# Linear attention with a mixture of adapters: v copied with a one behind each token, and sums of 65 columns instead of 128

## The chip, the cores and the metric

The kernel runs on one core of a Trainium2 chip. The metric is the device time of one execution in microseconds (us). Below, PE is the matrix engine, DVE, ACT and POOL are the vector, scalar and GpSimd engines, SP is the engine that issues the stores.

## The reference

The program computes a linear ("cosformer") attention for 8 batches, 8 heads, 576 tokens and head size 64, and sends its output, as a matrix of 4608 tokens by 512, through a mixture of 8 low-rank adapters of which each token takes two:

```
q_p = concat(relu(q) * cos_w, relu(q) * sin_w)      # 128 features a head
k_p = concat(relu(k) * cos_w, relu(k) * sin_w)
kv  = einsum('bhsf,bhsd->bhfd', k_p, v)
z   = sum over s of k_p
x   = einsum(q_p, kv) / (einsum(q_p, z) + 1e-06)    # x: (4608, 512)
logits = x @ w_gate;  topk = two best of 8;  w = softmax over the two
out = x + sum over the chosen e of w_e * (x @ A[e]) @ B[e]
```

## The kernel before, in words

A batch has 576 tokens as 64 rows of 9 slots s; two heads of 64 rows each fill the 128 partitions, so k, q and v of a batch are tiles of 128 x (4 head pairs, 9 slots, 64). Work is staged by a loop over 36 token tiles n of 128 tokens (`for n in range(NT - 1)`, L511), each of two slots of a batch; nine tiles make two batches, and the fifth of nine mixes both (`mixed`). The order of the instructions on every engine is written out by hand (`tc.manual_schedule`): in step n come, as far as they are due, `evac_x` (n-1), `normalise` (n), `move_q` (n+1), logits, the k-v sums, gates, deltas, `transp_x` (n), the k work and `numden` (n+1). Tables computed ahead (`kv_at`, `relu_at`, `pool_at`, `act_at`, `dve_at`, `gate_a_at` and so on) say which step does what.

- k: `relu_k` (L165, DVE, in place, bf16) and then `scale_k` (L156, POOL) by the cosine and the sine make `kp`, two instructions a slot. For batches 4 to 7 the relu pair and POOL's 16 or 18 instructions are issued in steps 12, 17, 20 and 23.
- k-v sums: `kv(b, s)` (L180) adds one slot of a batch to the sums in the two PSUM banks `cd`: 8 matmuls, 4 head pairs by two row halves of 64, with the 128 features of kp as weights. The moving side is 64 columns of v and 64 columns of one, which give z in 64 equal columns (`v_rhs` makes the two pieces by a jump to a block of ones behind v). `kv_out` (L188, ACT) takes 65 columns of each. For batch b the sums are spread over the steps ahead of its first tile: batches 4 to 7 in steps 14 to 17, 18 to 21, 23 to 26 and 27 to 30.
- q: `transp_q` (L213, or L201 from tile 27 on) transposes and scales q on PE, `evac_q` (L229, ACT) applies the relu.
- `numden(n)` (L247, L252) makes numerator and denominator of a tile, 65 columns a head; a first small matmul puts 1e-06 into the denominators. `normalise` (L259, L266, DVE) takes the reciprocal and multiplies into `xt`.
- `transp_x` (L274), `evac_x` (L280, DVE), `logits` (L300), `gate_a`, `gate_sig`, `gate_b`, `transp_z` (L348), `delta` (L366, L371) and `evac_o` (L397) are the adapters, in groups of three tiles.

A step's DVE list is: `evac_x`, `normalise`, gates, DVE's scales, `relu_k`. A step's PE list is: `transp_q`, logits that are early, `kv`, deltas, `transp_x`, `transp_z`, late logits, `numden` of the next tile.

Of the kernel before, what the change touches and what calls it, by code (L numbers as in the profile page):

```python
# [8 lines left out]
FP32 = mybir.dt.float32  # L9
BF16 = mybir.dt.bfloat16  # L10
AF = mybir.ActivationFunctionType
ALU = mybir.AluOpType

NS = 9
HALF = 64
EPS = 1e-6
# [3 lines left out]
def kernel(ctx, tc, q, k, v, w_gate, A, Bw, out):  # L20
    nc = tc.nc
    B, H, S, D = q.shape
# [4 lines left out]
    W = D + 1  # L27
    ZW = ER + R
    DCH = DM // 128
    G = H // 2  # L30
# [3 lines left out]
    persist = ctx.enter_context(tc.tile_pool(name="persist", bufs=1))  # L34
# [128 lines left out]
    def relu_k(b, s0, s1):  # L163
        x = k_b[b][:, :, s0:s1, :].rearrange("p g s d -> p g (s d)")
        nc.vector.tensor_scalar(out=x, in0=x, scalar1=0.0, scalar2=None, op0=ALU.max)  # L165

    def v_rhs(b, g, s, pr):
        base = v_b[b][pr, (g * NS + s) * D:(g * NS + s + 1) * D]
        p, (step, n) = base.ap[0], base.ap[-1]
        jump = VN - (g * NS + s) * D  # L170
        return bass.AP(base.tensor, base.offset, [p, [jump * step, 2], [step, n]])

    kv_n = {b: 0 for b in range(B)}

    def kv(b, s):
        first, last = kv_n[b] == 0, kv_n[b] == NS - 1
        kv_n[b] += 1
        for g in range(G):
            for par, pr in enumerate((lo, hi)):
                nc.tensor.matmul(out=kvz[par][:, g], lhsT=kp_t[b][pr, s, g],  # L180
                                 rhs=v_rhs(b, g, s, pr),
                                 start=(first and g == 0), stop=(last and g == G - 1))

    def kv_out(b):
        kv_t[b] = t = p_kv.tile([128, 2, G, W], BF16, name="kvsb")
        for par in range(2):
            src = kvz[par].rearrange("p g u d -> p g (u d)")[:, :, 0:W]
            nc.scalar.copy(t[:, par], src)  # L188
# [44 lines left out]
    def move_q(n):  # L233
        transp_q(n)
        evac_q(n, 0)
        evac_q(n, 1)

    def numden(n):
        nd_t[n] = nd = ps.tile([128, 2, 512], FP32, name="nd")
        tok = tokens(n)  # L240
        if mixed(n):
            jobs = [(lo, tok[0][0]), (hi, tok[1][0])]
        else:
            jobs = [(slice(0, 128), tok[0][0])]
        for gg in range(2):
            qpT = qpT_t.pop((n, gg))
            nc.tensor.matmul(out=nd[:, gg, D:4 * W:W], lhsT=ones, rhs=eps_hi, start=True,  # L247
                             stop=False, skip_group_check=True)
            for j in range(4):
                h = 2 * j + gg if quad(n) else gg * 4 + j  # L250
                for pr, b in jobs:
                    nc.tensor.matmul(out=nd[pr, gg, j * W:(j + 1) * W],  # L252
                                     lhsT=qpT[:, j, pr], rhs=kv_t[b][:, h % 2, h // 2, :],
                                     start=False, stop=(j == 3), skip_group_check=True)

    def normalise(n):
        nd = nd_t.pop(n)[:, :, 0:4 * W].rearrange("p g (j x) -> p g j x", x=W)
        rden = p_g.tile([128, H], FP32, name="rden")
        nc.vector.reciprocal(rden, nd[:, :, :, D:W])  # L259
        xt_t[n] = xt = p_x.tile([128, DM], BF16, name="xt")  # L260
        x = xt
        if quad(n):
            x = xt.rearrange("p (g two d) -> p two g d", two=2, d=D)
        else:
            x = xt.rearrange("p (g j d) -> p g j d", g=2, d=D)
        nc.vector.tensor_tensor(  # L266
            out=x, in0=nd[:, :, :, 0:D],
            in1=rden.rearrange("p (g j) -> p g j", g=2).to_broadcast([128, 2, 4, D]),
            op=ALU.mult)
# [18 lines left out]
    def logits(n):  # L288
        g = group_of[n]
        i = n - groups[g][0]  # L290
        if i == 0:
            if g == len(groups) - 1:
                t = qd.tile([128, 512], FP32, name="zb", tag="qd")
            else:
                t = ps.tile([128, 512], FP32, name="za")
            za_t[g] = t[:, 0:3 * ZW].rearrange("p (i z) -> p i z", z=ZW)
            u_t[g] = t[:, 3 * ZW:3 * ZW + 3 * E].rearrange("p (i e) -> p i e", e=E)
        xT = xT_t.pop(n)
        for c in range(DCH):
            nc.tensor.matmul(out=za_t[g][:, i, :], lhsT=xT[:, c, :], rhs=AW[:, :, c, :],  # L300
                             start=(c == 0 and i == 0), stop=(c == DCH - 1),
                             skip_group_check=True)
# [107 lines left out]
            (eng or nc.sync).dma_start(out=dst, in_=t)  # L410


    kv_at, relu_at, pool_at, act_at, dve_at = {}, {}, {}, {}, {}

    def put(at, step, what):
        at.setdefault(step, []).append(what)
# [6 lines left out]
    for b in range(2, B):  # L423
        first = b // 2 * NS + b % 2 * 4
        at = {2: 5, 3: 8, 4: 12, 5: 17, 6: 20, 7: 23}[b]
        n_pool = {2: 5, 3: 7, 4: 8, 5: 8}.get(b, 9)
        for s0, s1 in ((0, 3), (3, n_pool)):
            put(relu_at, at, (b, s0, s1))
        for s in range(n_pool):
            put(pool_at, at, (b, s))  # L430
        for i in range(2):
            if n_pool <= 7:
                put(dve_at, at, (b, 7, i))
            if n_pool < 9:
                put(act_at, first - 4 + i, (b, 8, i))
            if n_pool == 5:
                put(act_at, first - 3 + i, (b, 6, i))
                put(act_at, first - 2, (b, 5, i))
        order = (7, 0, 1, 2, 3, 4, 8, 6, 5) if n_pool <= 7 else (0, 1, 2, 3, 4, 5, 8, 6, 7)
        if n_pool == 9:  # L440
            order = range(NS)
        for j, s in enumerate(order):

            ahead = (2 if j < 4 else 1) if b < 4 else 4 - min(j // 2, 3)
            put(kv_at, first - ahead, (b, s))


# [2 lines left out]
    prev = 5  # L450
    for g, t in enumerate(groups[:-2]):
        at = max(t[-1] + 1, prev + 1)
        if g == 1:
            at += 1
        for n in t:
            if t[-1] + 1 < at or (n < t[-1] and prev == at - 1):
                put(late_at, at - 1, n)
            else:
                put(early_at, max(n + 1, at - 1), n)
        prev = at + 1  # L460
        put(gate_a_at, at, g)
        put(gate_b_at, at + 1, g)
        put(move_at, at + 2, g)
    put(late_at, NT - 2, NT - 3)

    with tc.manual_schedule():
# [44 lines left out]
        for n in range(NT - 1):  # L511
            if n > 0:
                g = move_at.get(n - 1, (None,))[0]
                evac_x(n - 1, g)
                if g is not None:
                    todo += groups[g]
            normalise(n)
            if n != 3:
                move_q(n + 1)
            for t in early_at.get(n, ()):  # L520
                logits(t)
            for b, s in kv_at.get(n, ()):
                kv(b, s)
                if kv_n[b] == NS:
                    kv_out(b)
            if n == 3:
                move_q(n + 1)
            for g in gate_a_at.get(n, ()):
                gate_a(g)
            for g in gate_b_at.get(n, ()):  # L530
                gate_b(g)
            now = todo[:2 if len(todo) > 3 and n not in kv_at else 1]
            del todo[:len(now)]
            for d in now:
                emit(d, n not in kv_at, add=n > 27)
            for g in gate_a_at.get(n, ()):
                gate_sig(g)
            transp_x(n)
            for g in move_at.get(n, ()):
                transp_z(g)  # L540
            for b, s, i in dve_at.get(n, ()):
                scale_k1(b, s, i, "dve")
            for b, s0, s1 in relu_at.get(n, ()):
                relu_k(b, s0, s1)
            for b, s in pool_at.get(n, ()):
                scale_k(b, s)
                if (b, s) == pool_at[n][-1]:
                    if b + 3 < B:
                        load_k(b + 3)
                    if b + 2 < B:  # L550
                        load_q(b + 2)
                    if b + 3 < B:
                        load_v(b + 3)
                    if b + 3 == B - 1:

                        nc.sync.dma_start(out=first_loads, in_=k_b[B - 1][0:1, 0, 0, 0:8])
                        for d in held:
                            store(d)
                        held = None
            for t in late_at.get(n, ()):  # L560
                logits(t)
            numden(n + 1)
            for b, s, i in act_at.get(n, ()):
                scale_k1(b, s, i, "act")
# [57 lines left out]
```

## Time and profile before

| | |
|---|---|
| time, median of 3 runs | 115.53 us (115.42 to 115.57) |
| the profiled execution | 115.39 us |
| its span | 113.6 us, 5022 instructions |
| busy | PE 99.4, DVE 80.9, ACT 78.1, POOL 73.2 us |
| kv matmuls (L180) | 576, 20.1 us busy |
| HBM | 28.85 MB read, 9.44 MB written |

The page gives the busy time of each engine, then the span in 40 slices, the DMA queues, the chain of work that ended last, and the costliest groups of instructions. In a timeline row stand start, length, engine, line, operation, output<-inputs, shape and count; an instruction's length counts from its start on the engine to its end, and neighbours overlap by some tens of ns. Rows of stretches give, for each engine, busy time and number of instructions, then the granted PE clock, the DMA share and GB/s.

### The profile page before, as it was taken

The page shows a single profiled execution, that of the slowest core. Times are in us where ns is not written, and L with a number is a line of the kernel's source. Part 1 is how long each engine was busy: PE and PEld are TensorE (multiplying, and loading weights), DVE is VectorE, ACT ScalarE, POOL GpSimd, SP SyncE. Part 2 cuts the span into 40 slices and gives each one's busy share as a digit, 9 for nine tenths or more (in the row PEclk, how much of TensorE's full clock was granted, in tenths as well). Part 3 has the DMA queues.
Part 4 walks back from the last instruction along what each step waited for, and adds up shares of the span by engine and source line. Part 5 has one row for each costly group of instructions (what it writes and reads, how often), then busy time and mean ns, then how long its engine had stood idle before and what let it go on. Part 6 is the DMA issues. An engine that isn't in the chain of part 4 may idle for free.

```text
span 113.6 us, 5022 instructions
## 1 busy us (share of the span) xinstructions
PE 99.4 (88%) x2099; PEld 74.2 (65%) x2099; DVE 80.9 (71%) x280; ACT 78.1 (69%) x169; POOL 73.2 (64%) x135
## 2 busy tenths in 40 slices
PE   2999777877898999999999999999999999978710
PEld 1347566766795688777877877777877876754200
DVE  5698488559949958696767886998658478786620
ACT  5077579846995847586876958956777678895720
POOL 5991222238996994999449989989950444984000
PEclk9999999999999999999999999999999999999998
DMA  2999999999999999999999999999988122655892
GB/s 40 383 208 207 207 209 207 208 184 211 204 214 203 206 209 209 208 208 209 207 209 206 211 204 208 260 359 378 380 304 314 52 97 98 175 190 220 291 332 88
DMA packets 19671, 24.77 MB, mean 218 GB/s; under 512 B 2625, under 2 KB 14529, under 8 KB 19649
## 3 DMA queue, kind: packets, MB, share of 16 engines
q0 software_dynamic: 13856, 13.84, 73.2%
q1 hardware_dynamic: 5792, 10.62, 26.4%
q8 instruction: 16, 0.26, 0.9%
q14 instruction: 7, 0.05, 0.1%
HBM read 28.85 MB, written 9.44 MB: 337 GB/s over the span
## 4 chain that ended last, share of the span: by engine, by line
PE 52%; DMA 26%; DVE 11%; POOL 3%; issue 2%; ACT 2%; POOLq 0%; DVEq 0%; ACTq 0%
DMA k<-in_k_dram 14%; DMA v<-in_v_dram 12%; PE cd L180 10%; PE za L300 8%; PE qd L213 7%; PE nd L252 6%; PE xz L274 5%; PE dx L366 4%; DVE xt L266 4%; PE qd L201 3%; PE dx L371 3%; PE xz L348 2%; DVE zg L335 2%; DVE xT L280 2%; ACT qpT L229 1%
## 5 line engine op out<-in xcount | busy, mean ns | idle before, releaser
L229 ACT ACTIVATE qpT<-qd 128x512 bf16<-128x512 f32 x71 | 38.6, 596 | 15.2 <-PE qd L213 11.5
L156 POOL TENSOR_SCALAR kp<-k,cos_tab 128x256 bf16<-128x256 bf16 x46 | 22.5, 490 | 7.2 <-DVE k L165 6.3
L280 DVE COPY xT<-xz 128x512 bf16<-128x512 bf16 (+1 forms) x36 | 17.2, 477 | 13.7 <-PE xz L348 7.5
L266 DVE TENSOR_TENSOR xt<-nd,rden 128x512 bf16<-128x512 f32 x36 | 24.9, 691 | 1.4
L156 POOL TENSOR_SCALAR kp<-k,sin_tab 128x256 bf16<-128x256 bf16 x46 | 21.9, 476 | 0.0
L180 PE MATMUL cd<-v,kp 64*128 64x128 bf16 x576 | 20.1, 217 | 0.8 <-DMA v<-in_v_dram 0.8
L274 PEld LDWEIGHTS <-xt 128*128 128x128 bf16 x144 | 10.8, 115 | 12.0 <-DVE xt L266 7.6
L180 PEld LDWEIGHTS <-kp 64*128 64x128 bf16 x576 | 16.2, 94 | 3.4 <-issue 0.8
L252 PE MATMUL nd<-kvsb,qpT 128*128 128x65 bf16 (+1 forms) x320 | 16.9, 194 | 1.0 <-DVE qpT L231 0.5
L274 PE MATMUL xz<-ident,xt 128*128 128x128 bf16 x144 | 14.4, 222 | 3.6 <-DVE xt L266 3.6
L213 PE MATMUL qd<-diag,q 128*64 128x128 bf16 x432 | 17.2, 222 | 0.0
L391 POOL TENSOR_TENSOR osb<-osb,xt 128x512 f32<-128x512 f32 x9 | 10.2, 1160 | 9.5 <-ACT osb L397 9.0
L397 ACT COPY osb<-dx 128x512 f32<-128x512 f32 x18 | 10.6, 591 | 5.3 <-PE dx L371 5.0
L213 PEld LDWEIGHTS <-q 128*64 128x64 bf16 x432 | 12.9, 109 | 1.5 <-DMA q<-in_q_dram 0.2
L252 PEld LDWEIGHTS <-qpT 128*128 128x128 bf16 (+1 forms) x320 | 12.4, 99 | 1.7 <-ACT qpT L229 0.7
L300 PE MATMUL za<-AW,xT 128*128 128x144 bf16 x140 | 12.2, 227 | 0.6 <-DVE zg L335 0.5
L247 PE MATMUL nd<-eps_hi,ones 128*128 128x4 bf16 x72 | 11.6, 169 | 0.0
L300 PEld LDWEIGHTS <-xT 128*128 128x128 bf16 x144 | 9.1, 98 | 2.8 <-DVE xT L280 0.8
L259 DVE RECIPROCAL rden<-nd 128x8 f32<-128x8 f32 x36 | 7.2, 200 | 4.8 <-PE nd L252 4.8
L397 ACT COPY osb<-cd 128x512 f32<-128x512 f32 x17 | 9.7, 599 | 1.3 <-PE cd L371 1.3
L62 POOL DMA_DIRECT2D v<-in_v_dram x8 | 6.3, 782 | 5.1 <-DMA q<-in_q_dram 4.3
L471 PE MATMUL wu<-wide,ones 128*128 128x512 bf16 x24 | 7.7, 495 | 2.0 <-DVE AW L115 2.0
(73 smaller groups left out, 137.5 us busy)
## 6 DMA issues: line engine op xcount, KB each, us to landing
out_dram<-osb SPq DMA_DIRECT2D x32, 256.0 KB, 3.9
v<-in_v_dram POOLq DMA_DIRECT2D x8, 576.0 KB, 17.2
q<-in_q_dram POOLq DMA_DIRECT2D x8, 576.0 KB, 16.2
k<-in_k_dram POOLq DMA_DIRECT2D x7, 576.0 KB, 15.6
k0f<-in_k_dram SPq DMA_DIRECT2D x1, 1152.0 KB, 5.4
out_dram<-osb SPq DMA_DIRECT2D x8, 128.0 KB, 2.5
AW<-in_moe_A_dram POOLq DMA_DIRECT2D x1, 128.0 KB, 18.1
Ball<-in_moe_B_dram POOLq DMA_DIRECT2D x1, 128.0 KB, 16.5
```

What stands on the lines that cost most here:

```text
L156: nc.gpsimd.tensor_scalar(out=dst, in0=src, scalar1=tab, scalar2=1.0, op0=ALU.mult, op1=ALU.mult)
L180: nc.tensor.matmul(out=kvz[par][:, g], lhsT=kp_t[b][pr, s, g], rhs=v_rhs(b, g, s, pr), start=(first and g == 0), stop=(last and g == G - 1))
L213: nc.tensor.matmul(out=t[cols, j, 2 * gi:2 * gi + 2, :], lhsT=q_b[b][:, 2 * gp + gi, s, :], rhs=diag[:, s, i], start=(j == 0 and gi == 0), ...
L229: nc.scalar.activation(t, src, AF.Relu)
L247: nc.tensor.matmul(out=nd[:, gg, D:4 * W:W], lhsT=ones, rhs=eps_hi, start=True, stop=False, skip_group_check=True)
L252: nc.tensor.matmul(out=nd[pr, gg, j * W:(j + 1) * W], lhsT=qpT[:, j, pr], rhs=kv_t[b][:, h % 2, h // 2, :], start=False, stop=(j == 3), sk ...
L266: nc.vector.tensor_tensor(out=x, in0=nd[:, :, :, 0:D], in1=rden.rearrange("p (g j) -> p g j", g=2).to_broadcast([128, 2, 4, D]), op=ALU.mult)
L274: nc.tensor.transpose(out=xz[:, c * 128:(c + 1) * 128], in_=x[:, c], identity=ident)
L280: nc.vector.tensor_copy(t[:, 0:c], xz[:, 0:c * 128].rearrange("p (c s) -> p c s", c=c))
L300: nc.tensor.matmul(out=za_t[g][:, i, :], lhsT=xT[:, c, :], rhs=AW[:, :, c, :], start=(c == 0 and i == 0), stop=(c == DCH - 1), skip_group_ ...
L391: nc.gpsimd.tensor_tensor(out=t, in0=t, in1=xt_t.pop(n), op=ALU.add)
L397: nc.scalar.copy(t, src)
```

## The change

- For batches 4 to 7 DVE copies v, two or three slots at a time, into one of three tiles `v1` whose slots have 66 columns, the last two of them one (set once by POOL in step 3). The copy of tokens' slots 0-1, 2-3, 4-5 and 6-8 of batch b stands at the end of DVE's list in the steps `first - 5` to `first - 2`, where `first` is the batch's first tile: steps 13 to 16, 17 to 20, 22 to 25 and 26 to 29. The matmuls of these batches then read 65 adjacent columns and write 65 instead of 128.
- In the 16 tiles of `kv_at` beyond 13 (14 to 21, 23 to 30) the 1e-06 is no longer put in by matmuls: DVE adds it to the denominators before the reciprocal.
- The k-v sums of batch 3 are spread over steps 10 to 12 instead of 11 and 12; group 1's gate is no longer held back a step, so that groups 1 to 3 are gated one step earlier (8, 10, 12 instead of 9, 11, 13); early logits stand behind `kv` instead of ahead of it.

```diff
+    VS = D + 2
+    v1_t = [persist.tile([128, G, 3, VS], BF16, name=f"v1{i}") for i in range(3)]
+    v1_of = {}
+
+    def copy_v(b, ss):
+        t = v1_t.pop(0)
+        v1_t.append(t)
+        src = v_b[b][:, 0:VN].rearrange("p (g s d) -> p g s d", g=G, s=NS)
+        nc.vector.tensor_copy(t[:, :, 0:len(ss), 0:D], src[:, :, ss[0]:ss[-1] + 1, :])
+        for i, s in enumerate(ss):
+            v1_of[b, s] = t[:, :, i, 0:W]
+
     def kv(b, s):
...
-                nc.tensor.matmul(out=kvz[par][:, g], lhsT=kp_t[b][pr, s, g],
-                                 rhs=v_rhs(b, g, s, pr),
+                o, rhs = kvz[par][:, g], None
+                if (b, s) in v1_of:
+                    o, rhs = cd[par][:, g * 128:g * 128 + W], v1_of[b, s][pr, g]
+                else:
+                    rhs = v_rhs(b, g, s, pr)
+                nc.tensor.matmul(out=o, lhsT=kp_t[b][pr, s, g], rhs=rhs,
                                  start=(first and g == 0), stop=(last and g == G - 1))
...
+    def eps_dve(n):
+
+        return n > 13 and n in kv_at
+
     def numden(n):
...
-            nc.tensor.matmul(out=nd[:, gg, D:4 * W:W], lhsT=ones, rhs=eps_hi, start=True,
-                             stop=False, skip_group_check=True)
+            if not eps_dve(n):
+                nc.tensor.matmul(out=nd[:, gg, D:4 * W:W], lhsT=ones, rhs=eps_hi, start=True,
+                                 stop=False, skip_group_check=True)
...
-                                     start=False, stop=(j == 3), skip_group_check=True)
+                                     start=(eps_dve(n) and j == 0), stop=(j == 3),
+                                     skip_group_check=True)
...
     def normalise(n):
...
-        nc.vector.reciprocal(rden, nd[:, :, :, D:W])
+        den = nd[:, :, :, D:W]
+        if eps_dve(n):
+            den1 = p_g.tile([128, 2, 4, 1], FP32, name="den1")
+            nc.vector.tensor_scalar(out=den1, in0=den, scalar1=EPS, scalar2=None, op0=ALU.add)
+            den = den1
+        nc.vector.reciprocal(rden, den)
...
+        if b >= 4:
+            for i in range(4):
+                put(copy_at, first - 5 + i, (b, range(2 * i, 2 * i + 2 + i // 3)))
         for j, s in enumerate(order):
 
-            ahead = (2 if j < 4 else 1) if b < 4 else 4 - min(j // 2, 3)
+            if b == 2:
+                ahead = 2 if j < 4 else 1
+            elif b == 3:
+                ahead = 3 if j < 2 else 2 if j < 5 else 1
+            else:
+                ahead = 4 - min(j // 2, 3)
             put(kv_at, first - ahead, (b, s))
...
-        if g == 1:
-            at += 1
...
             normalise(n)
+            if n == 3:
+                for t in v1_t:
+                    nc.gpsimd.memset(t[:, :, :, D:], 1.0)
             if n != 3:
                 move_q(n + 1)
-            for t in early_at.get(n, ()):
-                logits(t)
             for b, s in kv_at.get(n, ()):
                 kv(b, s)
                 if kv_n[b] == NS:
                     kv_out(b)
+            for t in early_at.get(n, ()):
+                logits(t)
...
             for b, s0, s1 in relu_at.get(n, ()):
                 relu_k(b, s0, s1)
+            for b, ss in copy_at.get(n, ()):
+                copy_v(b, ss)
             for b, s in pool_at.get(n, ()):
                 scale_k(b, s)
```

More of the change, by code (lines that the diff above doesn't have):

```diff
@@ L410, in store @@
             (eng or nc.sync).dma_start(out=dst, in_=t)
-    kv_at, relu_at, pool_at, act_at, dve_at = {}, {}, {}, {}, {}
+    kv_at, relu_at, pool_at, act_at, dve_at, copy_at = {}, {}, {}, {}, {}, {}
     def put(at, step, what):
```

## The prediction

> **What bounds the kernel now.** I read the page first (busy times, slices, chain), then the busy time by stretches, then the timeline of DVE and POOL inside the longest stretch.
>
> ```profile
> PE 99.4 (88%) x2099; PEld 74.2 (65%) x2099; DVE 80.9 (71%) x280; ACT 78.1 (69%) x169; POOL 73.2 (64%) x135
> PE 52%; DMA 26%; DVE 11%; POOL 3%; issue 2%; ACT 2%; POOLq 0%; DVEq 0%; ACTq 0%
> DMA k<-in_k_dram 14%; DMA v<-in_v_dram 12%; PE cd L180 10%; PE za L300 8%; PE qd L213 7%; PE nd L252 6%; PE xz L274 5%; PE dx L366 4%; DVE xt L266 4%; PE qd L201 3%; PE dx L371 3%; PE xz L348 2%; DVE zg L335 2%; DVE xT L280 2%; ACT qpT L229 1%
> ...
> core 0: us, PE busy (x) PEld busy (x) DVE busy (x) ACT busy (x) POOL busy (x), PEclk, DMA share, GB/s
> 34.30:49.13 14.83, 14.07 (x291) 10.89 (x290) 11.56 (x44) 9.65 (x22) 12.27 (x25) 1.00 1.21 207
> 49.13:94.09 44.96, 44.65 (x1020) 35.06 (x1020) 33.94 (x106) 33.02 (x71) 33.19 (x67) 1.00 1.00 240
> ```
>
> The first 34.3 us wait for loads (the chain's DMA share). From 49.13 to 94.09, which are steps 14 to 30 of the token-tile loop, 17 steps of 2.64 us, PE is busy 44.65 of 44.96 us: PE sets the pace, and DVE has 44.96 - 33.94 = 11.0 us to spare. Everything the change adds lies in this stretch, or one step ahead of it.
>
> POOL matters too. It scales k in four unbroken runs of `scale_k`, of 16, 16, 18 and 18 instructions, each released by the `relu_k` pair of the same batch on DVE (steps 12, 17, 20, 23):
>
> ```profile
> 45.55:53.02 7.47, 7.45 (x16) 1.00 1.22 210
> 58.28:65.76 7.48, 7.44 (x16) 1.00 1.21 208
> 66.80:75.17 8.37, 8.35 (x18) 1.00 1.18 246
> 75.60:83.90 8.30, 8.24 (x18) 1.00 1.02 375
> ```
>
> One relu of the fourth batch met the end of the third run. In the timeline of DVE and POOL:
>
> ```profile
> 45.11 0.35 DVE L165 TENSOR_SCALAR k<-k 128x768 bf16<-128x768 bf16 x1
> 57.85 0.35 DVE L165 TENSOR_SCALAR k<-k 128x768 bf16<-128x768 bf16 x1
> 58.12 0.49 DVE L165 TENSOR_SCALAR k<-k 128x1280 bf16<-128x1280 bf16 x1
> 58.30 0.64 POOL L156 TENSOR_SCALAR kp<-k,cos_tab 128x256 bf16<-128x256 bf16 x1 [3.06 <-DVE k L165]
> 58.93 0.47 POOL L156 TENSOR_SCALAR kp<-k,sin_tab 128x256 bf16<-128x256 bf16 x1
> 65.83 0.81 DVE L165 TENSOR_SCALAR k<-k 128x768 bf16<-128x768 bf16 x1
> 73.77 0.48 POOL L156 TENSOR_SCALAR kp<-k,sin_tab 128x256 bf16<-128x256 bf16 x1
> 73.79 1.58 DVE L165 TENSOR_SCALAR k<-k 128x768 bf16<-128x768 bf16 x1
> 74.22 0.48 POOL L156 TENSOR_SCALAR kp<-k,cos_tab 128x256 bf16<-128x256 bf16 x1
> 74.68 0.48 POOL L156 TENSOR_SCALAR kp<-k,sin_tab 128x256 bf16<-128x256 bf16 x1
> 75.65 0.53 POOL L156 TENSOR_SCALAR kp<-k,cos_tab 128x256 bf16<-128x256 bf16 x1 [0.49 <-PE xz L348]
> ```
>
> The same relu of 768 bf16 elements takes 0.35 us when POOL is idle and 1.58 us here. It ends at 75.37, which is 0.35 us after 75.03, 0.13 before the recorded end of the last POOL instruction of the run (75.16). Two POOL instructions, at 74.22 and 74.68, started after it and went first. The other way round, the POOL instruction at 58.30 that meets a running relu takes 0.64 instead of 0.47, so it waits for that one relu and no more. I read: a bf16 DVE instruction from SBUF to SBUF and a POOL instruction exclude each other, POOL gets in between two of DVE, and DVE gets in only where POOL's run has a gap. DVE's copies out of PSUM don't take part:
>
> ```profile
> 48.88 0.62 DVE L280 COPY xT<-xz 128x896 bf16<-128x896 bf16 x1
> 59.85 0.62 DVE L280 COPY xT<-xz 128x896 bf16<-128x896 bf16 x1 [1.24 <-PE xz L348]
> 67.60 0.62 DVE L280 COPY xT<-xz 128x896 bf16<-128x896 bf16 x1 [0.50 <-PE xz L348]
> 75.76 0.61 DVE L280 COPY xT<-xz 128x896 bf16<-128x896 bf16 x1
> 91.05 0.62 DVE L280 COPY xT<-xz 128x896 bf16<-128x896 bf16 x1 [1.50 <-PE xz L348]
> ```
>
> They take the same 0.62 us inside POOL's runs (48.88) and after the last of them (91.05).
>
> **The change part by part.** *Narrower k-v sums.* 288 of the 576 `kv` matmuls (batches 4 to 7) stream 65 columns instead of 128.
>
> ```profile
> 52.95 0.55 PE cd L180 x16
> 83.87 0.43 PE qd L201 x32
> 48.67 0.17 PE L247 MATMUL nd<-eps_hi,ones 128*128 128x4 bf16 x1
> 48.70 0.28 PE L252 MATMUL nd<-kvsb,qpT 128*128 128x65 bf16 x4
> 48.82 0.17 PE L247 MATMUL nd<-eps_hi,ones 128*128 128x4 bf16 x1
> ```
>
> Today one costs 0.55/16 = 34 ns. The nearest rows bound the new one: the 64x64 matmuls with 64 columns run at 0.43/32 = 13 ns, and the numerator's 65-column matmuls with a whole 128x128 weight load at 0.15/5 = 30 ns (from 48.67 to 48.82, one eps and four of them). With half the weight rows and full columns it lies between: 22 ns, 288 x 12 = 3.5 us of PE saved (bounds 1.2 to 6.0; 0 if the weight load sets the pace).
>
> *No eps matmul* in 16 tiles (n of 14 to 21 and 23 to 30): 32 of those 30 ns, 1.0 us of PE. In exchange a `tensor_scalar` of 128x8 from PSUM, in front of the reciprocal and on the path from `numden` to `xt`: the nearest row is the reciprocal itself.
>
> ```profile
> L259 DVE RECIPROCAL rden<-nd 128x8 f32<-128x8 f32 x17 | 3.4, 198 | 0.8 <-PE nd L252 0.8
> ```
>
> 16 x 0.2 = 3.2 us of DVE. *The copies* without hindrance: by the relu at 57.85 (the next starts 0.27 later) 0.2 us for 512 elements and 0.27 for 768: 12 x 0.2 + 4 x 0.27 = 3.5 us. DVE then needs 33.9 + 3.2 + 3.5 = 40.6 us in these 17 steps, 2.39 a step, and PE 44.65 - 4.5 = 40.1. The two are level and wait for each other every step, so I count 60% of PE's 4.5 us: -2.7 us (from +3.2, the eps adds wholly exposed with no gain, to -7.0).
>
> *Copies against POOL's runs.* `copy_v` stands at the end of DVE's list of a step, behind `relu_k`; behind it stand `evac_x` and `normalise` of the next step, for which PE's `transp_x` waits, and PE's next `kv` needs the copy itself. By the reading above:
> - Step 13 (batch 4, tokens 0 and 1): DVE reaches it by about 48.9, POOL's first run lasts to 53.01. DVE is free again at 53.01 - 0.13 + 0.2 = 53.08 instead of 48.88: **4.2 us**. The copies of steps 14 to 16 find POOL without a run.
> - Step 17: relu, relu, copy. POOL's first instruction already waits when the second relu ends, takes its turn, and 16 instructions follow to 65.75. DVE is free at 65.82 instead of 59.85: **6.0 us**. By then steps 18 and 19 have no run to meet.
> - Step 20: likewise with 18 instructions and a three-token copy: 75.16 - 0.13 + 0.27 = 75.30, but here the first relu took 0.81 instead of 0.35 (POOL was writing a load's descriptors, which will long be over): 74.84 instead of 67.60: **7.2 us**.
> - Step 23: the run to 83.89; its relu no longer waits 1.23 us, so 82.73 instead of 75.76: **7.0 us**. Steps 24 to 29 are free.
>
> Together 24.4 us, all exposed: PE has only the next `transp_q` to do meanwhile.
>
> The Trainium skill ("SBUF — State Buffer", Who interferes with whom) says that such a DVE instruction and a POOL instruction lock each other out, for the whole of the one instruction that issued first. By that rule a copy would wait for one scale of 0.45 us, and the sum would be rival C's 113.9. This trace's 1.58 us, across two later POOL instructions, disagrees.
>
> *PE's clock.* Half speed shows at both ends of the trace:
>
> ```profile
> 2.00:6.77 4.77, 4.77 (x12) 1.70 (x12) 1.00 1.01 291
> 6.78:9.60 2.82, 2.82 (x14) 1.08 (x12) 1.00 1.21 208
> ...
> 108.45:112.58 4.13, 0.00 (x0) 0.00 (x0) 0.69 (x1) 0.15 (x1) 0.00 (x0) 1.00 0.71 261
> 112.60:113.60 1.00, 0.00 (x0) 0.00 (x0) 0.00 (x0) 0.00 (x0) 0.00 (x0) 0.50 0.03 8
> ```
>
> After 4.13 us without a matmul the granted clock is 0.5; and in the first 4.77 us of the warm-up twelve 512-column matmuls run where later twelve need 2.6 us. (The column says 1.00 there because no clock event precedes.) Stall 1 leaves PE idle some 3.4 us, the others 5 to 7, so three of them should drop the clock, each for about 4.8 us of work, 2.4 us lost if PE is the bound throughout. I take half, 3 x 1.2 = **3.6 us** (0 to 9.6).
>
> *The rest.* The group-1 gate a step earlier, the batch-3 sums over three steps and logits behind `kv` reorder work of steps 7 to 15: PE has 14.83 - 14.07 = 0.8 us idle from 34.3 to 49.1; I take -0.3 (+0.3 to -0.8). Three small memsets on POOL lie under the load-bound start.
>
> Sum: the profiled execution took 115.39 us (span 113.6 and 1.79 around it; the three runs' median is 115.53). 115.4 - 0.3 - 2.7 + 24.4 + 3.6 = **140.4 us**. Own range 133 to 146.
>
> **The rivals.** *B, the copy goes first behind the relus.* If DVE keeps the port between two instructions in a row, the copies of steps 17, 20 and 23 pass, and those of the steps after meet the runs: step 13 4.2, step 18 about 3.6, step 22 about 2.9, step 24 about 5.8, in all 16.5, with one or two clock drops (1.5): 115.4 - 3.0 + 16.5 + 1.5 = 130.4 (124 to 134). Against it: the start of the trace, where POOL's descriptor writing gets between DVE's back-to-back diag builds, one of which then takes 0.51 instead of 0.26 us:
>
> ```profile
> 3.86 0.76 POOL L62 DMA_DIRECT2D k<-in_k_dram  x1
> 3.96 0.26 DVE L110 TENSOR_SCALAR diag<-ident,cos_tab 128x128 bf16<-128x128 bf16 x1 [1.49 <-POOL ident masks.py:199]
> 4.13 0.51 DVE L110 TENSOR_SCALAR diag<-ident,sin_tab 128x128 bf16<-128x128 bf16 x1
> ```
>
> *C, faster: DVE gets in at the next POOL boundary.* Then a copy waits at most one POOL instruction, 0.45, on average 0.23. Some nine copies fall into runs: 2.1 us more of DVE, 42.7 us in all, so that of 44.96 at most 2.3 can be won, less by the waits: I take 1.2, 115.4 - 0.3 - 1.2 = 113.9 (112 to 117). It decides where a copy in a run takes under some 0.6 us. For it: POOL itself waited for one relu only. Against it: the 1.58 us, across two boundaries.
>
> *D, faster: the copies don't contend,* as their rows of 64 differ from the relu's long rows: 115.4 - 0.3 - 2.7 = 112.4. Against it: same type, both ends in SBUF.
>
> *E, not what it says:* 65 columns save nothing as the weight load sets the pace; inside the forecast that is 2 us more, within its range.
>
> **How the numbers follow.** Forecast 0.50, B 0.22, C 0.22, D 0.06. A difference under 0.2% (0.23 us) can't be told from none. Slower: 0.72 from the forecast and B, and 0.05 of C, 0.77; same 0.02; faster 0.15 of C and D, 0.21. The range takes nearly all of the forecast and B and half of C: 113 to 146.
>
> **What would show it.** Right: four COPY instructions v1<-v of over 4 us in steps 13, 17, 20 and 23, each ending with POOL's last scale of a run, the other twelve near 0.3; PEclk under 1 behind them; `evac_x` idle before it. B: the long copies stand in steps 18, 22 and 24. C: none over 0.8 us. The narrow sums: 16 of them in about 0.35 us. Wrong altogether: time near 113 with DVE busy over 90% from step 14 to 30.

## The result, and the profile after

The changed kernel takes 114.41 us (median of 6 runs, 114.11 to 114.68) beside 115.55 us of the kernel before on the same chip (6 runs): a ratio of 0.990, interval 0.988 to 0.992. It is faster by 1.1 us; the forecast was 140.4. The profiled execution took 114.68 us, its span is 112.9.

Busy times and slices of DVE and PEclk from the page after, and the same stretch as before from the busy times by stretches:

```profile
PE 94.1 (83%) x2050; PEld 71.1 (63%) x2068; DVE 87.2 (77%) x312; ACT 78.5 (70%) x169; POOL 73.8 (65%) x137
DVE  5599489459969676798997999999989788777410
PEclk9999999999999999999999999999999999999997
POOL 11%; PE 11%; DVE 11%; ACT 3%; issue 2%; DMA 2%; DVEq 0%; ACTq 0%
49.00:94.00 45.00, 41.41 (x1025) 32.90 (x1034) 40.77 (x141) 34.41 (x74) 37.14 (x72) 1.00 1.04 249
49.80:92.60 42.80, 39.68 (x969) 31.37 (x973) 38.84 (x135) 32.76 (x69) 35.25 (x69) 1.00 1.05 252
```

Over the whole span PE's busy time fell by 5.3 us and DVE's rose by 6.3. In steps 14 to 30 (49.80 to 92.60) DVE is busy 38.84 of 42.80 us, 91%; before it was PE that was busy 99%. PE's granted clock never dropped before the end. The chain's shares are small because it could be followed back only to 62.29.

The groups of the new instructions in that stretch, and one row of the chain with 16 narrow sums:

```profile
L199 PE MATMUL cd<-v,kp 64*128 64x65 bf16 x288 | 7.9, 191 | 0.9 <-POOL kp L156 0.6 <-issue 0.3
L183 DVE COPY v<-v 128x512 bf16<-128x512 bf16 (+1 forms) x16 | 6.6, 415 | 0.0
L286 DVE TENSOR_SCALAR den<-nd 128x8 f32<-128x8 f32 x16 | 2.4, 152 | 0.0
83.65 0.35 PE cd L199 x16
```

The narrow sums run at 0.35/16 = 22 ns, the adds cost 0.15 us each, and the copies, waits included, 0.41. Two places of the timeline where DVE meets a run of POOL:

```profile
72.14 0.48 POOL L156 TENSOR_SCALAR kp<-k,cos_tab 128x256 bf16<-128x256 bf16 x1
72.23 0.54 DVE L183 COPY v<-v 128x512 bf16<-128x512 bf16 x1
72.60 0.52 POOL L156 TENSOR_SCALAR kp<-k,sin_tab 128x256 bf16<-128x256 bf16 x1
74.05 1.42 DVE L165 TENSOR_SCALAR k<-k 128x768 bf16<-128x768 bf16 x2
```

The copy at 72.23 (0.28 bare) waits for the rest of one scale, 0.25 us, and goes first at the next boundary; the scale behind it is held instead. Even the relu pair at 74.05, whose first is the relu of the forecast's 1.58 us, now gets through. No copy waited over 0.3 us. The stalls, 24.4 of the forecast's 25 us, were not there.

Three things were left to find: whether such a stall exists at all, what made the gain, and why it was not more.

### The profile page after: what moved, and what is told of

The parts are those of the page before. It is cut to its first block, busy times and chain, and to the rows that moved or that the text cites. A ratio compares the mean times of both kernels' runs of the same rounds, so it can differ in the third digit from the quotient of the medians.

```text
span 112.9 us, 4975 instructions
## 1 busy us (share of the span) xinstructions
PE 94.1 (83%) x2050; PEld 71.1 (63%) x2068; DVE 87.2 (77%) x312; ACT 78.5 (70%) x169; POOL 73.8 (65%) x137
## 5 line engine op out<-in xcount | busy, mean ns | idle before, releaser
L156 POOL TENSOR_SCALAR kp<-k,cos_tab 128x256 bf16<-128x256 bf16 x46 | 23.3, 506 | 6.4 <-DVE k L165 6.2
L199 PE MATMUL cd<-v,kp 64*128 64x128 bf16 (+1 forms) x576 | 17.5, 204 | 1.4 <-POOL kp L156 0.6
L199 PEld LDWEIGHTS <-kp 64*128 64x128 bf16 x576 | 13.8, 94 | 4.3 <-POOL kp L156 1.1
L420 POOL TENSOR_TENSOR osb<-osb,xt 128x512 f32<-128x512 f32 x8 | 9.2, 1159 | 8.4 <-ACT osb L426 6.8
L426 ACT COPY osb<-dx 128x512 f32<-128x512 f32 x19 | 11.2, 589 | 5.0 <-PE za L329 1.9
L426 ACT COPY osb<-cd 128x512 f32<-128x512 f32 x16 | 9.1, 597 | 1.3 <-PE cd L400 1.3
L506 PE MATMUL wu<-wide,ones 128*128 128x512 bf16 x24 | 7.2, 469 | 2.0 <-DVE AW L115 2.0
L62 POOL DMA_DIRECT2D q<-in_q_dram x8 | 6.1, 758 | 3.3 <-DMA k<-in_k_dram 3.1
L62 POOL DMA_DIRECT2D k<-in_k_dram x7 | 5.4, 771 | 4.1 <-DMA k<-in_k_dram 2.4
```

The source lines that it names most:

```text
L62: eng.dma_start(out=t, in_=rows(dram, b))
L156: nc.gpsimd.tensor_scalar(out=dst, in0=src, scalar1=tab, scalar2=1.0, op0=ALU.mult, op1=ALU.mult)
L199: nc.tensor.matmul(out=o, lhsT=kp_t[b][pr, s, g], rhs=rhs, start=(first and g == 0), stop=(last and g == G - 1))
L420: nc.gpsimd.tensor_tensor(out=t, in0=t, in1=xt_t.pop(n), op=ALU.add)
L426: nc.scalar.copy(t, src)
```

## Experiments: does DVE wait for the end of POOL's run?

**The copies alone.** The kernel before with `copy_v` at the same places, its tiles read by nobody.

```diff
+            for b, ss in copy_at.get(n, ()):
+                copy_v(b, ss)
```

> The kernel before, and in it the sixteen copies of v at their steps of the change, read by nobody; nothing else changed. Theory P (the prediction's: a copy that meets one of POOL's runs waits for the run's end): copies of over 4 us in steps 13, 17, 20 and 23, time near 135 us. Theory Q (a copy gets in at the next POOL boundary, as the changed kernel's trace suggests): no copy over 0.65 us, each met one taking its bare 0.28 or 0.35 plus what is left of the running scale less 0.13; time 115.5 to 117, since DVE had 11 us to spare.

115.42 us beside 115.43, ratio 0.9992 (0.9979 to 1.0006): the 16 copies alone cost nothing. The longest:

```profile
64.35 0.68 DVE L180 COPY v<-v 128x512 bf16<-128x512 bf16 x1
```

It came 0.08 us before a boundary, missed that one and took the next. So the forecast's reading of one row was not the rule.

**The 1e-06 by PE in every tile.** The changed kernel with

```diff
-        return n > 13 and n in kv_at
+        return False
```

> The changed kernel with the 1e-06 put in by PE's matmuls again in all tiles. Theory D (DVE sets the pace): 16 additions of 0.19 us start to start leave DVE, 3.0 us, against 1.0 us more of PE: 113.0 to 114.0. Theory PE (PE still sets it): 1 us later, 115.0 to 115.6. Neither: within 0.3 us of 114.4.

116.91 us is the middle of twelve runs in two groups, six from 114.99 to 116.46 and six from 117.36 to 117.71; the ratio of 1.003 (1.000 to 1.007) is that of the lower six. What parts the groups was not followed. The profiled run, 115.71, shows the forecast's stall for the first time:

```profile
71.95 3.33 DVE L183 COPY v<-v 128x512 bf16<-128x512 bf16 x1
```

This copy of step 22 waited 3.05 us, to the end of POOL's third run. So the comparison says nothing of the 1e-06; it is done again below.

**The old order.** The changed kernel with the gate of group 1, batch 3's sums and the early logits where they were before.

```diff
+        if g == 1:
+            at += 1
...
+            for t in early_at.get(n, ()):
+                logits(t)
             for b, s in kv_at.get(n, ()):
```

> The changed kernel with the order of before in the three places: group 1 held back, batch 3's sums in two steps, early logits ahead of kv. Theory H (the new order costs some 0.5 us ahead of step 14, where the changed kernel runs 0.5 to 0.8 us behind the one before, and this reaches the end): 113.7 to 114.1. Theory H0 (what is lost there is taken up later): 114.2 to 114.6. Theory H+ (the order is what makes the later steps fit): over 114.8.

118.03 us, ratio 1.022 (1.020 to 1.024): slower than before. The timeline, and the busy times behind it:

```profile
72.10 0.47 POOL L156 TENSOR_SCALAR kp<-k,cos_tab 128x256 bf16<-128x256 bf16 x1
72.11 3.79 DVE L183 COPY v<-v 128x512 bf16<-128x512 bf16 x1
75.27 0.47 POOL L156 TENSOR_SCALAR kp<-k,sin_tab 128x256 bf16<-128x256 bf16 x1
76.28 0.66 PE L329 MATMUL za<-AW,xT 128*128 128x144 bf16 x4 [2.93 <-DVE xT L309]
76.00:79.60 3.60, 3.32 (x39) 2.40 (x41) 2.48 (x8) 0.58 (x1) 1.80 (x4) 0.53 1.02 386
```

One copy let seven later scales pass. PE stood for 2.93 us, and its granted clock averaged 0.53 in the 3.6 us from 76.00 on: the whole mechanism of the forecast, at one place instead of four.

**Where in a scale the copy arrives.** The copies of the last two runs came 0.02 and 0.00 us after the start of a scale. Here a 128x128 memset stands in front of the old order's copy of step 22.

```diff
+                if n == 22:
+                    for _ in range(1):
+                        nc.vector.memset(late[:, 0:128], 0.5)
                 copy_v(b, ss)
```

> The changed kernel in the old order, which took 118.0 us, with one memset of 128x128 bf16 on DVE (0.14 us) ahead of the copy of step 22, whose copy took 3.79 us there, having arrived 1 ns after a POOL scale began. Theory R (a copy that arrives within some 20 ns of the beginning of a scale, while two scales overlap, waits for the run's end; any other waits for the next boundary): the copy of step 22 takes under 0.6 us, no stall, 113.7 to 114.6 us, though some 0.1 us of work was added. Theory H+ (the old order itself costs it): 118.0 or a little more.

118.19 us, ratio 1.026 (1.021 to 1.032). The copy came 0.145 us into a scale and waited all the same:

```profile
72.30 3.64 DVE L185 COPY v<-v 128x512 bf16<-128x512 bf16 x1
```

The moment of arrival is not the cause. PE stood for 2.93 us here too, and its clock was halved for 3.41 us (first row); in the 1e-06 run above, where the copy left PE without a matmul for 2.55 us, the clock stayed at 1.00 (second and third row):

```profile
77.74:81.15 3.41, 3.41 (x52) 2.55 (x49) 2.94 (x13) 1.60 (x3) 3.31 (x7) 0.50 1.02 383
```

```profile
72.88:75.43 2.55, 0.00 (x0) 0.03 (x1) 2.55 (x2) 0.96 (x2) 2.25 (x5) 1.00 1.14 293
75.43:79.00 3.57, 3.57 (x81) 2.98 (x82) 3.40 (x11) 1.57 (x3) 2.00 (x5) 1.00 1.07 374
```

A second try at the moment of arrival put four small memsets ahead of step 13's copy in the kernel with the copies alone:

```diff
+                if n == 13:
+                    for _ in range(4):
+                        nc.vector.memset(late[:, 0:1], 0.5)
```

> The kernel before with the copies alone (115.42 us, no copy over 0.68 us), and four memsets of 128x1 on DVE ahead of the copy of step 13. That copy arrived 279 ns after a scale began, and scales begin every 453 to 454 ns; four memsets of 44 ns should bring it to 279 + 176 - 453 = 2 ns after the next. Theory R: it waits for the end of POOL's first run at 53.0, 3.9 us, and the time is 118 to 120. Any other arrival: at most 0.75 us, time 115.4 to 115.7.

The copy came 0.24 us into a scale of the first run, missed the aim, and took 0.38 us; one run of 115.83 us. It tells nothing more.

**POOL's descriptors ahead of the run.** Only the third run directly follows the writing of a load's descriptors (q of batch 7). This load was issued with the loads behind the first run, in the old order, in the new order without the rest of the change, in the changed kernel and in before.

```diff
-                    if b + 2 < B:
+                    if b + 2 < B - 1:
                         load_q(b + 2)
...
+                    if b == 4:
+                        load_q(7)
```

> The changed kernel with the old order, whose copy of step 22 waited 3.5 us in POOL's third run; here the last load of q (batch 7) is issued with the loads behind POOL's first run instead of between its second and third, so that POOL writes no descriptors right ahead of the third run. Theory S (the descriptors written right ahead of a run are what leaves no turn for DVE between its scales): the copy of step 22 takes at most 0.6 us, the third run's first scale is 0.64 or more as in the runs that follow an idle POOL, no granted clock under 0.99, and the time falls from 118.0 to 115.2 to 116.0. Rival (the third run starves DVE whatever stands ahead of it): the copy of step 22 takes over 3 us again, 117.8 to 118.4.

> The kernel before with the new order alone, and the same load of q issued behind POOL's first run. Theory S: the relu of step 23, which took 1.73 us in the order alone, takes at most 0.7; the wait lay partly beside other work, so the time is 113.5 to 114.1. Rival: the relu takes over 1.2 us again, and 114.0 to 114.3; or the queue's other order makes a load late, 114.5 or more with idle time of PE before step 14.

> The changed kernel with the load of q of batch 7 issued behind POOL's first run. If the new order and the narrow sums relieve the same engine, so that their gains do not add once DVE is 91% busy: within 0.3 us of the changed kernel, 114.1 to 114.7, and behind the old order with the same early load (113.87). If the early load by itself is worth something besides the stall: 113.2 to 113.8. No long wait in POOL's third run by either, as its first scale is held by a relu and a copy already.

> The kernel before with the load of q of batch 7 issued behind POOL's first run, and nothing else. If the early load is worth nothing by itself, all that the old order with copies and narrow sums won (113.87) is theirs: 115.2 to 115.7 here. If the early load carries it: 114.0 to 114.6. The relu of step 23, 1.58 us in before, may wait or not; it is not on the path of this kernel by either.

The old order gained 4.2 us, more than either theory allowed: 113.87 us, ratio 0.987 (0.985 to 0.988), and its copy of step 22 (first row below) waited 0.23 us. But with the order alone the relu of step 23 (second row) still waited 0.98 us, to the end of the run; 114.82 us, 0.993 (0.990 to 0.995). That is 0.75 us behind the order alone, but not in all runs: three of the seven lie at 114.10 to 114.18, beside the order alone, and four at 114.82 to 114.96. In the profiled run, one of the four, the tiles fall behind at steps 29 to 31, which was not followed further.

```profile
71.86 0.51 DVE L183 COPY v<-v 128x512 bf16<-128x512 bf16 x1
```

```profile
73.58 1.33 DVE L165 TENSOR_SCALAR k<-k 128x768 bf16<-128x768 bf16 x1
```

In before with the early load the same relu still waited 0.77 us. So the descriptors are not the cause, though moving them took the wait away once. The changed kernel did not move: 114.43 us, 0.992 (0.990 to 0.995), though its last tile's xt came 0.84 us earlier. Before gained 0.16 us: 115.28 us, 0.9987 (0.9978 to 0.9996).

**The hold of the run's first scale.** Where the first scale of the third run took 0.77 us or more, held by relu and copy, nothing waited long. So one kernel got a hold (the order alone, with one unread copy behind the relus of step 20), and one lost it (the changed kernel, step 20's copy ahead of the relus):

```diff
+        if b == 6:
+            put(copy_at, at, (b, range(6, 9)))
```

```diff
+            if n == 20:
+                for b, ss in copy_at[n]:
+                    copy_v(b, ss)
             for b, s0, s1 in relu_at.get(n, ()):
                 relu_k(b, s0, s1)
-            for b, ss in copy_at.get(n, ()):
-                copy_v(b, ss)
+            if n != 20:
+                for b, ss in copy_at.get(n, ()):
+                    copy_v(b, ss)
```

> The kernel before with the new order alone, and one copy of three slots of v (read by nobody) behind the relus of step 20. Theory T (in POOL's third run DVE finds no turn where the run's first scale was held by one relu or none, 0.48 to 0.66 us, and finds one at every boundary where relu and copy held it, 0.77 or more): the first scale takes 0.8 us, the relu of step 23 at most 0.7 instead of 1.73, and the time is 113.8 to 114.1. Rival (the lengths of the first scale are chance): the relu takes over 1.2 us again, 114.1 to 114.3.

> The changed kernel with step 20's copy ahead of that step's two relus instead of behind them, so that one relu alone holds the first scale of POOL's third run. Theory T: that scale takes 0.65 us, the copy of step 22 or the relu of step 23 then waits to the end of the run, 1.2 to 3.6 us, and the time is 115.0 to 118.0. Rival: no copy over 0.7 us, and the time within 0.3 us of the changed kernel's 114.4.

With the hold (0.84) the relu of step 23 waited 0.21 us, as the theory expected; 114.16 us, 0.990 (0.987 to 0.993). Without it (0.64, first row) the copy of step 22 (second row) waited under 0.1 us all the same; 114.19 us, 0.991 (0.988 to 0.994):

```profile
67.26 0.64 POOL L156 TENSOR_SCALAR kp<-k,cos_tab 128x256 bf16<-128x256 bf16 x1 [0.33 <-PE xz L377]
71.78 0.36 DVE L183 COPY v<-v 128x512 bf16<-128x512 bf16 x1
```

That theory falls too. What decides stays open. Over all 20 traces, 160 relus and copies started inside a scale with over 0.13 us of it left: 152 waited at most 0.33 us, which is at most the rest of that scale less 0.13 us; 8 waited 0.77 to 3.5 us, to the run's end, all in POOL's third run. These 8 came 0.00 to 0.32 us into a scale.

## Experiments: what made the gain, and what held it back

**The order alone.** The kernel before with the three moves of the order, and no copies, narrow sums or adds; and with the logits behind the sums alone.

```diff
-        if g == 1:
-            at += 1
...
-            for t in early_at.get(n, ()):
-                logits(t)
             for b, s in kv_at.get(n, ()):
...
+            for t in early_at.get(n, ()):
+                logits(t)
```

> The kernel before with the new order alone (group 1's gate a step earlier, batch 3's sums over steps 10 to 12, early logits behind kv); no copies, sums of 128 columns, eps on PE. By the comparison of xt's starts, where the changed kernel is 0.5 us late at steps 12 and 13: 115.8 to 116.2. If the order pays later on (kv_out earlier): 115.0 to 115.4.

> The kernel before with the early logits behind the k-v sums, and nothing else of the new order. If this edit makes the order's gain of 1.4 us (PE has the sums to do while DVE makes xT, so that logits do not hold it up, every step): 114.0 to 114.4. If the gain comes from the gate of group 1 a step earlier and batch 3's sums over three steps: 115.2 to 115.6. A split: between.

The order alone takes 114.07 us (114.06 to 114.12), 0.988 (0.987 to 0.990): the miss of these runs, 1.4 us where 0.3 was forecast, and no less than the whole change. The logits alone give 114.38 us, 0.991 (0.990 to 0.993). PE's rows of one step show how, first before, then with the logits behind:

```profile
60.03 0.64 PE L213 MATMUL qd<-diag,q 128*64 128x128 bf16 x16
60.60 0.42 PE L300 MATMUL za<-AW,xT 128*128 128x144 bf16 x4
60.96 0.62 PE L180 MATMUL cd<-v,kp 64*128 64x128 bf16 x16
61.51 0.39 PE L366 MATMUL dx<-xt,ident 128*128 128x512 bf16 x1
```

```profile
59.79 0.64 PE L213 MATMUL qd<-diag,q 128*64 128x128 bf16 x16
60.36 0.62 PE L180 MATMUL cd<-v,kp 64*128 64x128 bf16 x16
60.92 0.42 PE L300 MATMUL za<-AW,xT 128*128 128x144 bf16 x4
61.18 0.38 PE L366 MATMUL dx<-xt,ident 128*128 128x512 bf16 x1
```

From the first `transp_q` to the first delta the same 36 matmuls take 1.48 us before and 1.39 behind. The four logits are followed after 0.36 us by the sums, but after 0.26 us by the deltas. The size of the weights stands in each row with a star (`128*64`, `64*128`, `128*128`). Where it changes from one matmul to the next, the two start 0.13 to 0.16 us apart where neither waits; the last logits and the first delta, both `128*128`, start 0.06 us apart. So the new order saves one change of three. In the eleven such steps between the xt of tiles 15 and 31 these intervals come to 5.16 us before and 3.88 us behind, a difference of 1.28, and PE's time from the one xt to the other falls by 1.26, from 42.07 to 40.81.

Waiting for xT, as the expectation had it, is a small part: in eight of the eleven steps the logits of before follow at the same 0.13 to 0.15 us although xT had been written 0.13 to 1.02 us earlier; in three they start 0.06 us behind the end of xT, up to 0.11 us late.

PE counts as busy as before all the same (44.55 of 45.00 us with the order alone, next fence), since the modelled ends of matmuls cover these intervals; the last tile's xt comes 1.34 us earlier. What the gate and batch 3's sums add, 0.3 us, was not taken apart.

```profile
49.00:94.00 45.00, 44.55 (x1065) 36.09 (x1063) 34.59 (x109) 34.04 (x74) 35.81 (x71) 1.00 1.04 248
```

**No copies.** The changed kernel, but the narrow sums read 65 adjacent columns of v itself, so that the denominators of batches 4 to 7 are sums of other columns of v:

```diff
-            for b, ss in copy_at.get(n, ()):
-                copy_v(b, ss)
...
-                if (b, s) in v1_of:
-                    o, rhs = cd[par][:, g * 128:g * 128 + W], v1_of[b, s][pr, g]
+                if b >= 4:
+                    c = (g * NS + s) * D
+                    o, rhs = cd[par][:, g * 128:g * 128 + W], v_b[b][pr, c:c + W]
```

> The changed kernel without the copies: the 65 columns are read straight from v, so that the column of one is a column of v instead (the denominators of batches 4 to 7 are left wrong). Theory D (DVE, 91% busy from step 14 to 30, took the place of PE and eats the gain): without 6.6 us of copies 112.3 to 113.2 us. Theory E (the path numden - den - reciprocal - xt sets the step, and the copies lie beside it): 114.1 to 114.5. If the copies' hold on POOL matters (POOL's runs end later, and PE waits for kp), 112.8 to 113.6.

113.5 us, 0.982 (0.979 to 0.985). Copies that cost nothing in before cost 0.9 us here. There DVE had room (37.33 of 45.00 us busy with them), here it has less (36.87 without them, 40.77 with them). That this is the reason is not shown: 113.5 lies in the range given for the copies' hold on POOL, not in Theory D's, and PE's weight loads wait 1.1 us for kp with the copies and 0.6 without.

**The 1e-06, priced without a stall.** The old order with the early load of q, and the 1e-06 by PE.

```diff
-        return n > 13 and n in kv_at
+        return False
```

> The old order with copies, narrow sums and the early load of q (113.87), the 1e-06 put in by PE's matmuls in every tile instead of by DVE in 16. If DVE is the engine that sets the pace there, 16 adds of 0.15 us fewer are worth up to 2.4 us on it, against 1.0 us more on PE: 112.8 to 113.6. If PE and DVE are level: 113.6 to 114.2. If a copy falls into a long wait in the third run: 115 or more.

113.57 us (113.08 to 113.97), 0.985 (0.983 to 0.987): faster than before and than the changed kernel, and but for the kernel without copies the lowest median of all. The two kernels of this comparison, with the adds and without:

```profile
49.00:94.00 45.00, 42.08 (x1023) 32.81 (x1031) 41.10 (x142) 33.92 (x74) 35.58 (x68) 1.00 1.01 242
```

```profile
49.00:94.00 45.00, 43.51 (x1101) 34.11 (x1097) 38.98 (x128) 34.60 (x76) 35.73 (x69) 1.00 1.02 243
```

Two us less on DVE and 1.4 more on PE brought the last xt 0.75 us earlier (100.60 against 101.35), but in the fastest of the four runs; the medians differ by 0.3, and the intervals overlap (0.987 is 0.985 to 0.988 with the adds). So the adds on DVE brought no gain; that they were a loss is likely and not shown.

**POOL's late slots.** Slot 8 of batches 6 and 7 by ACT, in the changed kernel, in the order alone, and in the old order with the early load:

```diff
-        n_pool = {2: 5, 3: 7, 4: 8, 5: 8}.get(b, 9)
+        n_pool = {2: 5, 3: 7}.get(b, 8)
```

> The changed kernel with slot 8 of batches 6 and 7 scaled by ACT, as it is for batches 4 and 5, so that POOL's last two runs have 16 instructions instead of 18. If POOL's runs have become a bound (the chain has POOL kp for 9.7%, and PE waits for kp in two places): 113.3 to 114.1. If DVE alone is the bound: 114.3 to 114.7. A copy may also fall into the narrow window, then 116 to 118.

> The kernel before with the new order alone, and slot 8 of batches 6 and 7 scaled by ACT instead of POOL (as of batches 4 and 5), so that POOL's third and fourth runs have 16 scales instead of 18. If these runs hold up the sums: 113.4 to 113.9. If nothing waits for them in this order, or ACT's four more instructions cost what POOL's save: 113.9 to 114.4.

> The old order with copies, narrow sums and the early load of q (113.87), and slot 8 of batches 6 and 7 on ACT, so that POOL's third and fourth runs are two scales shorter. If the sums of batch 6 and 7 wait for POOL's late slots there: 113.2 to 113.7. If the stores at the end set the time from there on: 113.7 to 113.9 with the last tile's xt earlier by 0.3 us or more. If the shorter run shifts a DVE instruction into a long wait: 115 or more, with one copy or relu over 1.2 us in the third run.

114.14 us, 0.989 (0.987 to 0.990); 114.75 us, 0.993 (0.989 to 0.997); 113.77 us, 0.986 (0.984 to 0.987). The second lies above both of its ranges; its five runs, like those of the order with the early load, fall apart into 114.16 to 114.17 and 114.75 to 115.14, and why was not followed. In the third the last tile's xt came only 0.05 us earlier, so these slots held nothing up there. In the changed kernel with the slot on ACT the last tile's xt came 2.10 us earlier than before, 0.75 more than in the changed kernel, but the median is lower by only 0.3 and the intervals overlap. The last stores that SP issues show a part of the rest (x4, total length); first changed, then changed with the early load, then the old order with it:

```profile
106.08 2.78 SPq L439 DMA_DIRECT2D out_dram<-osb  x4
```

```profile
105.23 2.89 SPq L439 DMA_DIRECT2D out_dram<-osb  x4
```

```profile
105.84 2.56 SPq L439 DMA_DIRECT2D out_dram<-osb  x4
```

In four kernels (changed, with the slot on ACT, with the early load, with the copy ahead of the relus) the last store but one took 0.78 to 0.90 us to issue instead of 0.57, and the span ended 5.06 to 5.25 us after the last copy out of PSUM instead of 4.45 to 4.64 in the other 16 kernels, before among them. Each is one execution of its kernel. Why these four was not tried.

## Why the prediction was wrong, point by point

- **Copies against POOL's runs, 24.4 us.** This is the step that failed: four times 4 to 7 us in the forecast, none in the changed kernel. A general rule was read out of one row, the relu at 73.79. The runs show such waits as the exception, 8 of 160, and at one place, the third run. The rows that spoke against it stood in the same trace only as POOL's side; no other relu of before met a run's middle, so one event carried 24 us. Rival C, the turn at the next boundary, was the right one. The Trainium skill ("SBUF — State Buffer", Who interferes with whom) says that such a DVE instruction and one of POOL lock each other out for the whole of the one that issued first. Here 152 of the 160 agree (at most 0.33 us, where a scale takes 0.47), 8 do not.
- **PE's clock, 3.6 us.** Without stalls this term was nothing. Where a stall did come, with the old order, wait and clock together made 118.03 - 113.87 = 4.2 us, 0.16 of it worth the early load by itself. That is 0.7 us more than DVE's wait of 3.5, and 1.2 more than the 2.93 us that PE stood; 1.2 a stall was forecast, so its size is not shown to be wrong. The half clock lasted 3.41 us instead of the 4.8 taken, and it came after 2.93 us without a matmul, while the forecast let a stall of 3.4 us pass without it.
- **Narrower sums and PE's gain.** The 22 ns are what was measured; they were chosen between two bounds, so the exact hit is luck. With the old order and no stall, copies, sums and adds together gave 115.28 - 113.87 = 1.4 us, where -2.7 was forecast (of at most 4.5); with the 1e-06 on PE 1.7.
- **The adds.** 0.15 us each instead of 0.2. DVE's total in steps 14 to 30, forecast 40.6, is 38.84, and PE's, forecast 40.1, is 39.68. That the two would be level, and gains on PE partly lost, held; the adds brought no gain that the runs show.
- **The rest, -0.3 us.** The term most in error after the stalls: the order gives 1.4 us by itself. It was put down to work of steps 7 to 15 and sized by PE's idle time there, 0.8 us. But the early logits move in steps up to 30, and the gain came in steps 14 to 30, where PE had looked full: one change of weight size less a step, 0.1 us each time.
- **The sum for rival C** (113.9) came near 114.41 by luck, with both of its parts wrong: -0.3 for the order was -1.4, and -1.2 for the rest was +0.3 on top of the order. Together the two gains of 1.4 us made 1.1: the last tile's xt comes 1.35 us earlier than before, no more than with the order alone, while DVE is at 91%, and the span ends 0.6 us later behind the last copy out of PSUM. That the full DVE is the reason for the first is not shown; with the early load as well the last xt comes 2.2 us earlier than in before with it.
- **The other rivals.** B named step 22 as a place of its stalls and 2.9 us as its price; with the old order 3.5 us stood there, at one place of its four; that DVE keeping its turn is what makes it is not shown. D falls by the waits of 0.25 us, E by the 22 ns.
- **What would show it.** "Time near 113 with DVE busy over 90%" was the mark for wrong altogether, and 114.41 with 91% is close to it.

## What to carry to other kernels

A cost that rests on one event of a trace is a bound, not a rule: weigh it with a chance, however well that one row fits a mechanism. When one engine is 99% busy by modelled ends, its order can still be worth more than the instructions that one takes off it: look at the starts of neighbouring matmuls of different kinds, and put those of one weight size next to each other. Two gains need not add once a second engine is near 90%. Before putting a small instruction on an engine, ask which engine is the fuller one after the change, not before it.

## What the runs showed of the hardware

- Of 160 relus and copies on DVE that met a scale of POOL with over 0.13 us of it left, 152 went in at the next boundary and waited at most that rest less 0.13 us. Of 17 with 0.13 us or less left, 14 went in at once and 3, with 0.07 to 0.09 us left, missed one boundary (0.39 to 0.41 us).
- In POOL's third run alone a relu or copy may find no turn until the run ends (3.05, 3.36 and 3.50 us for copies, 0.77 to 1.38 for relus). Neither the moment of arrival, nor descriptors ahead of the run, nor the hold of its first scale decides it; the cause is open.
- Two matmuls in a row whose weights differ in size (128x64, 64x64, 64x128, 128x128) started 0.10 to 0.16 us apart where neither waited for another engine; two kinds of matmul with one weight size and up to 144 columns, such as logits and delta, 0.03 to 0.06 us.
- PE's granted clock was halved for 3.41 us in two kernels that left it without a matmul for 2.93 us, and stayed at 1.00 after 2.55 us.
